# A recurrent-attention kernel: the carried state in a zero-padded layout, output matmuls all 64 columns wide, the two halves interleaved, and one gate moved forward on VectorE

## The chip, the cores and the metric

The kernel runs on one core of one Trainium2 chip. In the profiles PE is TensorE, DVE VectorE, ACT ScalarE and POOL GpSimd. The metric is the time of one execution on the device in microseconds (us), median over runs. The kernel before ran in 234.27 us (three runs, 232.32 to 235.18) when the prediction was made. One core has no second die to compare with, so a run counts as slow only where its time is over 1.5% above the fastest of its kernel; a single run is of unknown state. The figures inside one execution come from profiled executions; their span is about 1.8 us shorter than the time that is reported for the same run.

## The reference, cut to what matters

Per batch and head, a 48 x 48 state decays by `alpha`, takes in an outer product, and is read by `q`. The 384 outputs of a token (8 heads x 48) then go through a feed-forward layer with the activation h cos h.

```python
batch, n_heads, seq, head_dim = (4, 8, 768, 48)
for t in range(S):
    state = alpha[:, :, t, :, None] * state + np.einsum('bhd,bhe->bhde', k[:, :, t], v[:, :, t])
    y[:, :, t] = np.einsum('bhd,bhde->bhe', q[:, :, t], state)
...
h = x @ w_in          # 384 -> 2048
g = h * np.cos(h)
return (g @ w_out)    # 2048 -> 384
```

## The kernel before

The sequence is cut in 24 chunks of 128 tokens, 6 per batch. The recurrence within a chunk becomes matmuls; only the state goes from chunk to chunk. Head pairs share 128 contraction rows (two heads in slots of 64, 48 of them used). The state of a pair is 96 columns wide, so the state of all heads is 384 columns without gaps, the same layout as the output.

The output of a chunk is a 384 x 128 block, in three row groups (`kt`) of 128 partitions. Two sorts of matmul add up in it: the old state `U` against `q` ("U reads"), and `v` against the masked scores `A` ("v reads"). A v read is always 64 columns wide. A U read must not cross a pair, that is a multiple of 96, nor a 64-column tile, and so half of the U reads are only 32 columns wide:

```python
def state(j):                                   # "S": sum of k v over the chunk, plus the carry
    ...
    if not first:
        nc.tensor.matmul(t[:, 0 : NP * 96], ident_bf,
                         U_t[j - 1].rearrange("r p e -> r (p e)"), start=False, stop=True, ...)

def ev_state(j):                                # "u", on DVE
    t = work.tile([C, NP, 96], BF, tag="U_sb", bufs=3)
    nc.vector.tensor_tensor(out=t..., in0=U_ps.pop(j)..., in1=Em_t.pop(j)..., op=ALU.mult)
    U_t[j] = t

def outputs(j):                                 # "Y"
    ...
    for kt in range(3):
        if not first:
            U = U_t[j - 1].rearrange("r p e -> r (p e)")
            r = 0
            while r < C:
                f = kt * C + r
                p = f // 96
                n = min(96 * (p + 1), (kt + 1) * C, f - f % 64 + 64) - f     # 64 or 32
                mm(r, n, kt, U[:, f : f + n], qT[:, (NP + p) * C : (NP + p + 1) * C], True, False)
                r += n
        for r in range(2):
            for half in range(2):
                ...
                mm(64 * half, 64, kt, vs[:, c0 : c0 + 64],
                   A_t[j][:, ACOL[h] * C : (ACOL[h] + 1) * C], first and r == 0, r == 1)
```

The order in which each engine gets its work is written by hand, as a string of one-letter units per step. A step `s` works on chunk `s + 1` of the recurrence and on chunk `s` and `s - 2` of the feed-forward layer:

```python
units = {
    "T": transposes, "t": ev_transposes,        # TensorE; copy to SBUF on DVE
    "S": state, "u": ev_state,                  # TensorE; DVE
    "A": scores, "m": mask_scores,              # TensorE; DVE
    "Y": outputs, "y": ev_outputs,              # TensorE; DVE
    "0": ff1 first half, "1": ff1 second half,  # TensorE
    "i": act 0, "j": act 1,                     # ScalarE (sine)
    "p": gate 0, "r": gate 1,                   # DVE
    "2": ff2 first half, "3": ff2 second half, "e": ev_ff2, ...
}
elif s % 2 == 0:
    run(s, "o Tt 0i Su Am 2 1j Yyp r 3 e")
else:
    run(s, "o Tt 0i Su Am 2 1jp Yy r Pn 3 e C x")
```

## Time and profile before

| what | before |
|---|---|
| time | 234.27 us (232.32 to 235.18) |
| span of the profiled run | 235.5 us (its time was 237.25) |
| TensorE busy | 89% |
| one pair of steps without a first chunk (99.80 to 116.40 us) | 16.6 us |
| one output block of 20 matmuls, to the start of the next group | 1187 ns |
| wait of TensorE in each even step | 483 ns |

The profiled run, at 237.25 us, is 2.1% above the fastest run (232.32 us).

These lines are from the profile page of the kernel before: busy time by engine, the 40 slices of the span (tenths busy; PEclk is the granted TensorE clock in tenths), and the chain that ended last, by engine and by line.

```profile
span 235.5 us, 6142 instructions
PE 210.1 (89%) x2632; PEld 154.6 (66%) x2632; DVE 136.0 (58%) x160; ACT 124.7 (53%) x137; POOL 62.9 (27%) x104
...
PE   7858744877999999999999999999999999999983
...
PEclk9995985597999999999999999999999999999999
DMA  7999998991754777377268476843861561001001
...
PE 70%; DVE 18%; DMA 4%; ACT 2%; SPq 2%; issue 2%; ACTq 0%
```

From slice 11 on (about 60 us) TensorE stands at 9 and paces the kernel. The first 60 us have full DMA and a clock that comes and goes. DVE, on the chain with 18%, is busy for only 58% of the span, so the chain must hit it at a bad place. The timeline of DVE in an even step, and the longest wait of TensorE in the waits view (total us, times, longest), show where:

```profile
104.43 0.56 DVE L288 CAST t<-t 128x384 bf16<-128x384 f32 x1 [2.50 <-PE t L262]
104.90 2.35 DVE L317 TENSOR_TENSOR g_new<-t,c_sb 128x1024 bf16<-128x1024 f32 x2
107.16 0.68 DVE L199 COPY t<-t 128x1024 bf16<-128x1024 bf16 x1
...
PE t L233 <- DVE t L199: 7.4, 11, 3.7
```

DVE idles 2.5 us for the output block (unit Y), then runs y, both gates p and r, and only then the copy of the transposes (L199), for which the state matmuls (L233) wait. In nine even steps L233 starts 539 ns after the last ff1 matmul, where the matmul rate gives 56 ns.

The output block itself in the timeline of TensorE (start, length, instruction; the ends of matmuls are modelled, so read the starts):

```profile
103.14 0.41 PE L262 MATMUL t<-t 128*64 128x128 bf16 x3
103.47 0.30 PE L262 MATMUL t<-t,vpb 128*64 128x128 bf16 x4
103.61 0.22 PE L262 MATMUL t<-t 128*64 128x128 bf16 x2
103.66 0.28 PE L262 MATMUL t<-t,vpb 128*64 128x128 bf16 x4
103.87 0.41 PE L262 MATMUL t<-t 128*32 128x128 bf16 x3
104.04 0.35 PE L262 MATMUL t<-t,vpb 128*64 128x128 bf16 x4
104.32 1.47 PE L326 MATMUL o_new<-w_114,g_new 128*128 128x384 bf16 x8
```

The view merges neighbours (its first row holds one 64-wide and two 32-wide matmuls). The start stamps of the single matmuls in the same trace are finer. Columns: start in us, ns since the start before, width in columns, and what it is.

```
102.986   +55   128   (ff1)
103.136  +150    64   U
103.309  +173    32   U
103.312    +3    32   U
103.472  +160    64   v
103.476    +4    64   v
103.552   +76    64   v
103.556    +4    64   v
103.608   +52    64   U
...
103.872  +149    32   U
103.876    +4    32   U
104.036  +160    64   U
...
104.323  +152   128   (ff2)
```

Two matmuls on different halves start 3 or 4 ns apart, and the next pair follows 56 ns after. Every change of width takes 149 to 173 ns from start to start, and the first pair of 64-wide ones after it is followed by the next after 80 ns instead of 56. There are four changes inside the block (64 to 32 to 64, twice) besides the one into it and the one out of it.

### The profile page before, as it was taken

The numbers are of one execution on the slowest core, as the hardware profiler recorded it, in microseconds if no ns is written. First come the engines' busy times: TensorE is split into PE (matmuls) and PEld (weight loads), VectorE is DVE, ScalarE is ACT, GpSimd is POOL, SyncE is SP. The second block draws the span as 40 slices with busy tenths as digits, with TensorE's granted clock in tenths as the row PEclk, the third lists the DMA queues.
The fourth block names the chain that finished last, engine by engine and source line by source line (L and its number), as shares of the span: only waits on it lengthen the run. The fifth ranks groups of instructions, "written<-read, shape, count | busy, mean of one in ns | idle before, by whom it ended". The sixth has DMA issues, their size and how long they took to land.

```text
span 235.5 us, 6142 instructions
## 1 busy us (share of the span) xinstructions
PE 210.1 (89%) x2632; PEld 154.6 (66%) x2632; DVE 136.0 (58%) x160; ACT 124.7 (53%) x137; POOL 62.9 (27%) x104
## 2 busy tenths in 40 slices
PE   7858744877999999999999999999999999999983
PEld 2444642755786777777776867768777767778741
DVE  6535472293656738457557566486496566574620
ACT  4255407550594582863944945837729548323330
POOL 3220602650052080170250530800801605200000
PEclk9995985597999999999999999999999999999999
DMA  7999998991754777377268476843861561001001
GB/s 137 323 182 298 245 375 155 199 189 36 145 125 93 123 146 143 82 139 162 68 110 167 100 134 105 165 107 67 170 132 43 97 138 36 33 3 36 33 33 68
DMA packets 106203, 30.28 MB, mean 129 GB/s; under 512 B 100288, under 2 KB 105408, under 8 KB 106176
## 3 DMA queue, kind: packets, MB, share of 16 engines
q1 hardware_dynamic: 106176, 29.89, 59.5%
q8 instruction: 20, 0.33, 0.6%
q14 instruction: 7, 0.06, 0.1%
HBM read 25.17 MB, written 4.72 MB: 127 GB/s over the span
## 4 chain that ended last, share of the span: by engine, by line
PE 70%; DVE 18%; DMA 4%; ACT 2%; SPq 2%; issue 2%; ACTq 0%
PE o_new L326 23%; PE t L303 22%; DVE g_new L317 11%; PE t L262 11%; DMA a_new<-in_alpha_dram 4%; PE t L210 3%; PE t L193 3%; DVE t L199 3%; DVE t L288 3%; PE t L233 3%; PE cum_new L145 2%; PE t L239 2%; DVE w_114 L125 1%; DVE w_112 L115 1%; PE w_ps L338 1%
## 5 line engine op out<-in xcount | busy, mean ns | idle before, releaser
L310 ACT ACTIVATE c_sb<-t,halfpi 128x1024 bf16<-128x1024 f32 x48 | 53.5, 1114 | 63.1 <-PE t L303 62.7
L303 PE MATMUL t<-t,w_112 128*128 128x128 bf16 x1152 | 75.1, 224 | 1.0 <-DVE t L288 0.7
L326 PE MATMUL o_new<-w_114,g_new 128*128 128x384 bf16 x384 | 71.5, 331 | 3.9 <-DVE w_114 L125 2.8
L303 PEld LDWEIGHTS <-w_112 128*128 128x128 bf16 x1152 | 69.8, 100 | 4.5 <-DVE t L288 0.8
L317 DVE TENSOR_TENSOR g_new<-t,c_sb 128x1024 bf16<-128x1024 f32 x48 | 57.5, 1216 | 7.6 <-ACT c_sb L310 7.2
L174 POOL TENSOR_TENSOR khb<-t,icp_new 128x384 bf16<-128x384 f32 x24 | 24.0, 999 | 137.0 <-ACT icp_new L162 107.3
L326 PEld LDWEIGHTS <-g_new 128*128 128x128 bf16 x384 | 34.5, 98 | 28.3 <-issue 5.4
L288 DVE CAST t<-t 128x384 bf16<-128x384 f32 x24 | 13.4, 557 | 41.9 <-PE t L262 41.9
L219 DVE TENSOR_TENSOR t<-t,mask_f 128x1024 bf16<-128x1024 f32 x24 | 29.2, 1216 | 1.2 <-PE t L210 1.2
L331 ACT ACTIVATE o_sb<-o_new 128x384 f32<-128x384 f32 x24 | 11.6, 485 | 28.2 <-PE o_new L326 28.2
L245 DVE TENSOR_TENSOR t<-t,Em 128x384 bf16<-128x384 f32 x24 | 13.4, 558 | 21.3 <-PE t L239 17.2
L199 DVE COPY t<-t 128x1024 bf16<-128x1024 bf16 x24 | 16.5, 687 | 12.7 <-PE t L193 12.7
L176 POOL TENSOR_TENSOR qhb<-t,cp_new 128x384 bf16<-128x384 f32 x22 | 22.8, 1037 | 0.1
L262 PE MATMUL t<-t 128*64 128x128 bf16 (+1 forms) x160 | 21.2, 235 | 0.0
L262 PE MATMUL t<-t,vpb 128*64 128x128 bf16 x288 | 19.1, 229 | 0.0
L262 PEld LDWEIGHTS <-t 128*64 128x64 bf16 (+1 forms) x160 | 10.5, 102 | 7.5 <-issue 1.0
L233 PE MATMUL t<-vpb,khb 128*128 128x96 bf16 x96 | 8.5, 213 | 7.4 <-DVE t L199 7.4
L348 ACT ACT_TABLE_LOAD x11 | 14.1, 1283 | 0.9 <-PEq L448 0.7
L310 ACT ACT_TABLE_LOAD x11 | 14.1, 1283 | 0.2
L145 PE MATMUL cum_new<-lnab,triu_bf 128*128 128x384 bf16 x24 | 7.6, 343 | 7.3 <-ACT lnab L132 7.3
L132 ACT ACTIVATE lnab<-a_new 128x768 bf16<-128x768 f32 (+1 forms) x13 | 10.3, 793 | 6.4 <-DMA a_new<-in_alpha_dram 6.3
L178 POOL CAST vpb<-t 128x384 bf16<-128x384 f32 x24 | 13.1, 545 | 1.1 <-DMA t<-in_v_dram 0.6
(43 smaller groups left out, 145.4 us busy)
## 6 DMA issues: line engine op xcount, KB each, us to landing
a_new<-in_alpha_dram SPq DMA_DIRECT2D x24, 192.0 KB, 3.4
t<-in_k_dram SPq DMA_DIRECT2D x24, 192.0 KB, 3.8
t<-in_q_dram SPq DMA_DIRECT2D x24, 192.0 KB, 4.3
t<-in_v_dram SPq DMA_DIRECT2D x24, 192.0 KB, 4.2
out_dram<-o_sb SPq DMA_DIRECT2D x24, 192.0 KB, 2.0
w1f<-in_moe_w_in_dram SPq DMA_DIRECT2D x2, 1536.0 KB, 8.4
w2f<-in_moe_w_out_dram SPq DMA_DIRECT2D x2, 1536.0 KB, 10.9
```

Source lines behind the costliest of these rows:

```text
L174: nc.gpsimd.tensor_tensor(out=khb[:, j % 3, :, 0:D], in0=k_sb, in1=icp.rearrange("s (h d) -> s h d", h=H), op=ALU.mult)
L176: qeng.tensor_tensor(out=qhb[:, j % 3, :, 0:D], in0=q_sb, in1=cp[:, 0:HD].rearrange("s (h d) -> s h d", h=H), op=ALU.mult)
L199: nc.vector.tensor_copy(out=t, in_=qkT_ps.pop(j))
L219: nc.vector.tensor_tensor(out=t.rearrange("s (h t) -> s h t", h=H), in0=A_ps.pop(j).rearrange("s (h t) -> s h t", h=H), in1=mask_f.unsquee ...
L233: nc.tensor.matmul(t[:, p * 96 : (p + 1) * 96], khb[:, j % 3, 2 * p : 2 * p + 2].rearrange("s h d -> s (h d)"), vpb[:, j % 3, 2 * p : 2 * ...
L262: nc.tensor.matmul(t[r0 : r0 + n, kt * C : (kt + 1) * C], lhsT, rhs, start=start, stop=stop, skip_group_check=True)
L288: nc.vector.tensor_copy(out=t.rearrange("r k t -> r (k t)"), in_=y_ps.pop(j)[:, 0 : 3 * C])
L303: nc.tensor.matmul(t[:, f], w1[:, kk, ft * C : (ft + 1) * C], x_t[j][:, kk], start=(kk == 0), stop=(kk == 2))
L310: nc.scalar.activation(out=c_sb, in_=h_ps[j, half], func=AF.Sin, bias=halfpi, scale=1.0)
L317: nc.vector.tensor_tensor(out=g_t[j][:, half * HF : (half + 1) * HF], in0=h_ps.pop((j, half)), in1=c_t.pop((j, half)), op=ALU.mult)
L326: nc.tensor.matmul(o_ps[j][:, 0:DM], g_t[j][:, ft], w2[:, ft], start=(ft == 0), stop=(ft == NF - 1))
L348: nc.scalar.preload_act_table_set("natural_log_exp_and_others")
```

## The change

The state gets slots of 128 columns per pair, 96 used and 32 zero. A U read may then run over a pair's end into zeros, so all eight U reads can be 64 columns wide: a tile that spans two pairs is read twice, and each read adds zeros where the other has data. The number of matmuls stays 20. They are issued as two lists, one per half, in turn. In even steps the first gate p moves before the output block.

```diff
+    ub = consts.tile([C, 3, NP, C], BF, tag="ub")
+    nc.vector.memset(ub, 0.0)
...
     def ev_state(j):
-        t = work.tile([C, NP, 96], BF, tag="U_sb", bufs=3)
         nc.vector.tensor_tensor(
-            out=t.rearrange("r p (a e) -> r p a e", a=2),
+            out=ub[:, j % 3, :, 0:96].rearrange("r p (a e) -> r p a e", a=2),
...
+        U = ub[:, (j - 1) % 3].rearrange("r p e -> r (p e)")
+        mms = []
+        for T in range(2 * 3):
+            g, tt = T // 3, T % 3
+            a = []
             if not first:
+                for p, c0 in (((0, 0),), ((0, 64), (1, 96)), ((1, 160),))[tt]:
+                    c0 += 2 * C * g
+                    a.append((U[:, c0 : c0 + 64],
+                              qT[:, (NP + 2 * g + p) * C : (NP + 2 * g + p + 1) * C]))
             for r in range(2):
+                h = 4 * g + (2 * tt + r + 1) // 2
+                c0 = 4 * VS * g + 64 * (2 * tt + r)
+                a.append((vs[:, c0 : c0 + 64], A_t[j][:, ACOL[h] * C : (ACOL[h] + 1) * C]))
+            mms.append(a)
...
+        for i in range(max(len(mms[0]), len(mms[1]))):
+            for half in range(2):
+                if i < len(mms[half]):
+                    kt, start, stop, lhsT, rhs = mms[half][i]
+                    nc.tensor.matmul(t[64 * half : 64 * half + 64, kt * C : (kt + 1) * C], ...)
...
-            run(s, "o Tt 0i Su Am 2 1j Yyp r 3 e")
+            run(s, "o Tt 0i Su Am 2 1jp Yy r 3 e")
```

More of the change, by code (lines that the diff above doesn't have):

```diff
@@ L224, in mask_scores @@
         A_t[j] = t
-    U_ps, U_t = {}, {}
+    U_ps = {}
     def state(j):
@@ L238, in state @@
         if not first:
-            nc.tensor.matmul(t[:, 0 : NP * 96], ident_bf,
-                             U_t[j - 1].rearrange("r p e -> r (p e)"),
+            nc.tensor.matmul(t[:, 0 : NP * 96].rearrange("r (p e) -> r p e", p=NP), ident_bf,
+                             ub[:, (j - 1) % 3, :, 0:96],
                              start=False, stop=True, skip_group_check=True)
     def ev_state(j):
-        t = work.tile([C, NP, 96], BF, tag="U_sb", bufs=3)
         nc.vector.tensor_tensor(
-            out=t.rearrange("r p (a e) -> r p a e", a=2),
+            out=ub[:, j % 3, :, 0:96].rearrange("r p (a e) -> r p a e", a=2),
             in0=U_ps.pop(j)[:, 0 : NP * 96].rearrange("r (p a e) -> r p a e", p=NP, a=2),
@@ L249, in ev_state @@
         )
-        U_t[j] = t
     y_ps, x_t = {}, {}
@@ L259, in outputs @@
         qT = qkT_t[j]
-        def mm(r0, n, kt, lhsT, rhs, start, stop):
-            nc.tensor.matmul(t[r0 : r0 + n, kt * C : (kt + 1) * C], lhsT, rhs, start=start,
-                             stop=stop, skip_group_check=True)
-        for kt in range(3):
-            if not first:
-                U = U_t[j - 1].rearrange("r p e -> r (p e)")
-                r = 0
-                while r < C:
-                    f = kt * C + r
-                    p = f // 96
-                    n = min(96 * (p + 1), (kt + 1) * C, f - f % 64 + 64) - f
-                    mm(r, n, kt, U[:, f : f + n], qT[:, (NP + p) * C : (NP + p + 1) * C],
-                       True, False)
-                    r += n
-            for r in range(2):
-                for half in range(2):
-                    T = 2 * kt + half
-                    g, sl = T // 3, 2 * (T % 3) + r
-                    h = 4 * g + (sl + 1) // 2
-                    c0 = 4 * VS * g + 64 * sl
-                    mm(64 * half, 64, kt, vs[:, c0 : c0 + 64],
-                       A_t[j][:, ACOL[h] * C : (ACOL[h] + 1) * C], first and r == 0, r == 1)
+        U = ub[:, (j - 1) % 3].rearrange("r p e -> r (p e)")
@@ new lines, in outputs @@
+        for half in range(2):
+            mms[half] = [
+                (T // 2, i == 0, i == len(mms[T]) - 1) + m
+                for T in range(half, 6, 2) for i, m in enumerate(mms[T])
+            ]
+        for i in range(max(len(mms[0]), len(mms[1]))):
+            for half in range(2):
+                if i < len(mms[half]):
+                    kt, start, stop, lhsT, rhs = mms[half][i]
+                    nc.tensor.matmul(t[64 * half : 64 * half + 64, kt * C : (kt + 1) * C],
+                                     lhsT, rhs, start=start, stop=stop, skip_group_check=True)
@@ L291, in ev_outputs @@
         A_t.pop(j)
-        U_t.pop(j - 1, None)
     h_ps, g_t, o_ps = {}, {}, {}
```

## The prediction

> **What bounds the kernel.** From about 60 to 217 us TensorE sets the pace: in the 40 slices PE stands at 9, and the chain of waits runs mostly through it (PE 70%, DVE 18%). A pair of steps takes 16.6 us (state-carry matmul L239 at 99.80, then at 116.40). The first 60 us are mixed (DMA, casts, colder clock).
>
> **The output block (L262).** The starts of single matmuls in the trace show two 64-column matmuls on different halves starting 3 ns apart and pairs following every 56 ns; but where the column tile changes (128 to 64, 64 to 32, and back) the next start comes 149 to 173 ns later. The Trainium skill, "TensorEngine Tiling (Array Packing)", Key Properties, says that changing the tiling mode, not just the tile, drains the TensorE; the trace agrees. A 20-matmul block has four inner changes besides entry and exit; to the next group's start it takes 1187 ns in all 17 blocks after 62 us (timeline: 103.14 to 104.32). The 12-matmul block of a first chunk, all 64-column pairs already, takes 458 ns.
>
> **What changes.** (1) The 20 matmuls stay 20, all 64 columns wide, 10 per half, alternating. Estimate from the 458 ns block: 458 + 4 pairs x 56 = 682 ns. Each block saves 505 ns on the critical path: 17 blocks, 8.6 us. The three before 60 us give perhaps 0.9 us together.
> (2) In even steps DVE ran y, p, r and then the copy of the transposes (L199), which ended late: TensorE waits for it before L233 (waits view; 539 ns after the last ff1 matmul's start instead of 56, in 9 even steps: 4.3 us). With p before Y, p (1.22 us) runs while TensorE does ff1's second half, and the copy comes about 1.2 us earlier relative to Y, of which the shorter Y takes back 0.5 us. The wait should vanish: 4.3 us.
> (3) Added: a memset of the padded state on DVE, about 0.7 us (L69, equal size: 698 ns), before DVE waits 3.3 us for q: nothing. Strided state: nothing (L245 stays at 558 ns, L239 at 346 ns).
>
> **What could come back.** TensorE would need about 15.1 us per pair of steps; ACT and DVE are each busy a little over 10 us. The tightest chain: from odd steps ACT runs j, table load, ln, two exps, o_sb, table load, i without a break (111.52 to 119.0); then p on DVE. By my count p then ends just as y could start: at most 0.1 us of new wait a pair. DMA, busy 59.5% of the span, would reach 63%.
>
> **Sum.** 8.6 + 0.9 + 4.3 = 13.8 us, less 0.5 for new waits: 234.3 - 13.3 = 221.0 us. Range 218.5 to 224.0. Faster by over 2%: 0.96; within 2%: 0.03; slower: 0.01.
>
> **What the profile would show.** Right: L262 only as 128*64; 20-blocks of about 680 ns, no inner gap above 80 ns; no wait of L233 on L199 after 60 us; a pair of steps in 15.1 to 15.3 us; L245 and L239 unchanged; DVE below 10% of the chain. Wrong: blocks near 1 us (the halves do not overlap); a new wait of PE on L317, L288 or L199; a pair above 15.6 us.
>
> **What would make it wrong.** Accumulation from both halves at different column ranges of one bank serializing; the start shifting by a microsecond or two with the DMA; ACT or the input DMA not following the shorter step.

## The result, and the profile after

The changed kernel runs in 218.72 us (four runs, 218.52 to 220.73) against 234.73 us for the kernel before (four runs, 232.32 to 236.96; the slowest is 2.0% above the fastest, so it counts as slow, and the ratio is that of the other three). The ratio of the fast runs is 0.9369, with a 95% interval of 0.9270 to 0.9469. Such a ratio is the mean time of one kernel's fast runs over that of the other's of the same rounds, so it is not quite the ratio of the medians that are quoted. It is correct. The line numbers shift: L262 becomes L288 (output), L233 becomes L236 (state), L199 becomes L202 (copy), L303, L317 and L326 become L307, L321 and L330 (ff1, gates, ff2).

The same lines of the profile page as shown of before:

```profile
span 216.9 us, 6141 instructions
PE 193.0 (89%) x2630; PEld 147.9 (68%) x2632; DVE 135.9 (63%) x161; ACT 124.5 (57%) x137; POOL 62.4 (29%) x104
...
PE   6657653876999999999999999999999999999972
...
PEclk9999965699999999999999999999999999999999
DMA  7999999997765787489378575863863451101011
...
PE 82%; DVE 6%; DMA 4%; ACT 3%; SPq 2%; issue 2%; ACTq 0%; DVEq 0%
```

DVE falls from 18% of the chain to 6%, although it is busy as long as before (135.9 against 136.0 us). What remains in the chain is TensorE. The first, an inner and the last row of an output block, with the ff2 that follows:

```profile
101.91 0.25 PE L288 MATMUL t<-t,ub 128*64 128x128 bf16 x2
...
102.21 0.22 PE L288 MATMUL t<-t,vpb 128*64 128x128 bf16 x2
...
102.38 0.28 PE L288 MATMUL t<-t,vpb 128*64 128x128 bf16 x4
102.59 1.48 PE L330 MATMUL o_new<-w_116,g_new 128*128 128x384 bf16 x8
```

The block takes 681 or 682 ns in all 17 steady blocks (101.91 to 102.59). By the start stamps its inner gaps are 3 or 4, 77, and 52 or 53 ns, nothing longer. The even step on DVE, and the wait that remains:

```profile
94.44 1.23 DVE L321 TENSOR_TENSOR g_new<-t,c_sb 128x1024 bf16<-128x1024 f32 x1 [1.03 <-ACT c_sb L314]
95.58 0.55 DVE L293 CAST t<-t 128x384 bf16<-128x384 f32 x1
96.05 1.22 DVE L321 TENSOR_TENSOR g_new<-t,c_sb 128x1024 bf16<-128x1024 f32 x1
97.27 0.69 DVE L202 COPY t<-t 128x1024 bf16<-128x1024 bf16 x1
...
PE t L236 <- DVE t L202: 4.3, 2, 3.5
```

The gate p (94.44) now fills DVE's idle time before y (95.58). Of the eleven waits on the copy two remain, both before 60 us. The stretch from the fifth output block to the last one is the same work in both kernels, and the windows view of it (stretch, length, busy us of PE, PEld, DVE, ACT and POOL with numbers of instructions, clock, DMA share, GB/s) is the cleanest comparison. First before, then after:

```profile
62.53:216.97 154.44, 151.56 (x2060) 115.39 (x2058) 97.20 (x113) 93.40 (x101) 45.81 (x72) 1.00 0.52 105
```

```profile
57.03:198.94 141.91, 141.91 (x2060) 111.97 (x2059) 98.96 (x114) 93.32 (x101) 45.91 (x72) 1.00 0.56 114
```

The stretch is 12.53 us shorter, and by this view TensorE has no idle time left in it. The view goes by modelled ends, so short gaps like those at a change of width count as busy in both rows; the start stamps say the same of the wait, since the state matmuls now follow the last ff1 matmul by 55 or 56 ns in all 19 steps of the stretch. The tail after it is 0.51 us shorter (18.50 against 18.00 us), which is the last block. The first stretch, up to the fifth block, differs by 5.5 us in these two profiles (62.53 against 57.03 us); whether the change did that is a question for the experiments.

### The profile page after: what moved, and what is told of

The parts are those of the page before. It is cut to its first block, busy times and chain, and to the rows that moved or that the text cites. A ratio compares the mean times of both kernels' runs of the same rounds, so it can differ in the third digit from the quotient of the medians.

```text
span 216.9 us, 6141 instructions
## 1 busy us (share of the span) xinstructions
PE 193.0 (89%) x2630; PEld 147.9 (68%) x2632; DVE 135.9 (63%) x161; ACT 124.5 (57%) x137; POOL 62.4 (29%) x104
## 3 DMA queue, kind: packets, MB, share of 16 engines
q1 hardware_dynamic: 106176, 29.89, 64.6%
## 4 chain that ended last, share of the span: by engine, by line
PE 82%; DVE 6%; DMA 4%; ACT 3%; SPq 2%; issue 2%; ACTq 0%; DVEq 0%
PE o_new L330 30%; PE t L307 30%; PE t L288 7%; PE t L196 5%; DMA a_new<-in_alpha_dram 4%; PE t L213 3%; DVE g_new L321 3%; PE cum_new L148 2%; PE t L236 2%; PE t L242 2%; DVE t L222 1%; SPq L100 1%; PE cum_new L152 1%; ACT lnab L135 1%; DVE w_116 L128 1%
## 5 line engine op out<-in xcount | busy, mean ns | idle before, releaser
L307 PE MATMUL t<-t,w_114 128*128 128x128 bf16 x1152 | 73.9, 222 | 0.9 <-DVE t L293 0.9
L330 PE MATMUL o_new<-w_116,g_new 128*128 128x384 bf16 x384 | 70.3, 327 | 4.2 <-DVE w_116 L128 3.1
L307 PEld LDWEIGHTS <-w_114 128*128 128x128 bf16 x1152 | 68.9, 99 | 4.2 <-DVE t L293 1.1
L321 DVE TENSOR_TENSOR g_new<-t,c_sb 128x1024 bf16<-128x1024 f32 x48 | 58.4, 1218 | 18.1 <-ACT c_sb L314 17.7
L330 PEld LDWEIGHTS <-g_new 128*128 128x128 bf16 x384 | 34.2, 98 | 28.0 <-issue 4.9
L247 DVE TENSOR_TENSOR ub<-t,Em 128x384 bf16<-128x384 f32 x24 | 13.4, 558 | 23.9 <-PE t L242 18.7
L202 DVE COPY t<-t 128x1024 bf16<-128x1024 bf16 x24 | 16.6, 690 | 10.2 <-PE t L196 10.2
L179 POOL TENSOR_TENSOR qhb<-t,cp_new 128x384 bf16<-128x384 f32 x22 | 22.1, 1003 | 0.1
L293 DVE CAST t<-t 128x384 bf16<-128x384 f32 x24 | 13.3, 554 | 13.3 <-PE t L288 13.3
L288 PE MATMUL t<-t,vpb 128*64 128x128 bf16 x288 | 16.0, 224 | 0.4 <-DVE t L222 0.4
L288 PEld LDWEIGHTS <-vpb 128*64 128x64 bf16 x288 | 13.2, 112 | 0.7 <-issue 0.4
L288 PE MATMUL t<-t,ub 128*64 128x128 bf16 x160 | 13.4, 230 | 0.0
L152 PEld LDWEIGHTS <-lnab 128*128 128x128 bf16 x96 | 5.5, 98 | 10.9 <-issue 8.9
```

The lines of the kernel that those rows point to most:

```text
L179: qeng.tensor_tensor(out=qhb[:, j % 3, :, 0:D], in0=q_sb, in1=cp[:, 0:HD].rearrange("s (h d) -> s h d", h=H), op=ALU.mult)
L202: nc.vector.tensor_copy(out=t, in_=qkT_ps.pop(j))
L247: nc.vector.tensor_tensor(out=ub[:, j % 3, :, 0:96].rearrange("r p (a e) -> r p a e", a=2), in0=U_ps.pop(j)[:, 0 : NP * 96].rearrange("r ( ...
L288: nc.tensor.matmul(t[64 * half : 64 * half + 64, kt * C : (kt + 1) * C], lhsT, rhs, start=start, stop=stop, skip_group_check=True)
L293: nc.vector.tensor_copy(out=t.rearrange("r k t -> r (k t)"), in_=y_ps.pop(j)[:, 0 : 3 * C])
L307: nc.tensor.matmul(t[:, f], w1[:, kk, ft * C : (ft + 1) * C], x_t[j][:, kk], start=(kk == 0), stop=(kk == 2))
```

## The experiments

The theory has two independent parts: (a) TensorE pays for each change of column width, and (b) TensorE waited for a copy that stood behind a gate in the DVE queue. Rivals: the gain comes from the alternation of the halves or from the padding as such; the two parts overlap, or one wait only turns into another; the shorter first 60 us are part of the effect. The table gives all runs; the block is the steady output block of 20 matmuls, the pair is two steady steps, and the stretch goes from the fifth to the last output block.

| run | median us (runs) | ratio to before | block ns | pair us | stretch us | 5th block starts at us |
|---|---|---|---|---|---|---|
| before, first profile | 234.27 (3) | | 1187 | 16.59 | 154.44 | 62.53 |
| before_again | 234.39 (1) | | 1187 | 16.59 | 154.44 | 59.64 |
| changed kernel | 218.72 (4) | 0.9369 | 682 | 15.09 | 141.91 | 57.03 |
| after_again | 220.52 (4) | 0.9380 | 682 | 15.09 | 141.91 | 59.14 |
| order_only | 229.42 (5) | 0.9741 | 1187 | 16.10 | 150.00 | 60.26 |
| layout_only | 224.66 (4) | 0.9624 | 682 | 15.59 | 146.39 | 59.76 |
| tile_order | 220.33 (4) | 0.9401 | 682 | 15.09 | 141.91 | 60.02 |
| one_switch (wrong result) | 220.66 (4) | 0.9446 | 740 | 15.21 | 142.86 | 57.42 |
| one_switch_marks | 222.83 (1) | | 740 | 15.21 | 142.85 | 60.12 |
| three_switches | 226.89 (1) | | 1017 | 15.76 | 147.28 | 59.47 |
| half_by_half | 227.06 (1) | | 1043 | 15.81 | 148.14 | 58.75 |
| carry_dve | 217.92 (4) | 0.9275 | 682 | 14.76 | 139.31 | 58.66 |

One of the five runs of order_only and one of the four of tile_order, and two of the runs of before beside them, counted as slow by their time; the ratios leave these out, the medians in the table do not. Runs of one execution have no interval, so their times are not compared. All these verdicts rest on the block and the stretch, where the granted clock is 1.00 and which repeat to 0.02 us between profiles of the same kernel.

### Only the order of DVE's work

```diff
 (the kernel before)
-            run(s, "o Tt 0i Su Am 2 1j Yyp r 3 e")
+            run(s, "o Tt 0i Su Am 2 1jp Yy r 3 e")
```

> The kernel before with only the order in even steps changed (the gate of the first half before the output block). If the wait of the state matmuls on the copy of the transposes came from the gate's place in the DVE queue: the output block stays at 1187 ns, the gap from the last ff1 matmul to the state matmuls falls from 539 to about 56 ns in the 9 even steps, a pair of steps takes 16.6 - 0.48 = 16.1 us, and the time falls by about 4.3 us against the kernel before. Rival (the wait only moves to another buffer or engine): the pair stays near 16.6 us and the time within 1 us of before.

The block stays at 1187 ns, the steady wait is gone and the stretch falls by 4.44 us (154.44 to 150.00). The waits view of this run keeps only the two early waits:

```profile
PE t L233 <- DVE t L199: 4.3, 2, 3.5
```

The ratio is 0.9741 (0.9644 to 0.9839), that is 2.6% or some 6 us. The stretch's 4.44 us are 1.9% and lie inside the interval, so the surplus is no finding; the start, taken up below, varies by as much. Part (b) is shown alone, in its predicted size, and the wait did not move elsewhere.

### Only the layout and the width

```diff
 (the changed kernel)
-            run(s, "o Tt 0i Su Am 2 1jp Yy r 3 e")
+            run(s, "o Tt 0i Su Am 2 1j Yyp r 3 e")
```

> The changed kernel with the old order in even steps. If the two parts are independent: block 682 ns, the 483 ns wait of the state matmuls is still there in 9 even steps, a pair of steps takes 16.6 - 1.0 = 15.6 us, and the time is about 4.3 us above the changed kernel, 223 us. Rival (the shorter block alone already takes the wait away, or makes it longer because the copy now comes later against TensorE): a pair at 15.1 us, or above 15.9 us.

```profile
PE t L236 <- DVE t L202: 7.2, 11, 3.5
```

The block takes 682 ns, and all eleven waits on the copy are back. The stretch is 8.05 us shorter than before. The reason that the wait is neither longer nor shorter lies in the order: y, p, r and the copy on DVE all start from the end of the output block, and so does TensorE's work up to the state matmuls. A shorter block moves both sides by the same time: the state matmuls start 540 to 545 ns after the last ff1 matmul here, against 538 to 540 ns before. The two parts add up: 4.44 + 8.05 = 12.49 us against 12.53 us for both together. The median lies 5.9 us above the changed kernel's first 218.72 us, but that also holds a difference of starts; the stretch gives 4.48 us.

### Sixty-four columns, but in the old order of tiles

```diff
 (the changed kernel, outputs)
-        for i in range(max(len(mms[0]), len(mms[1]))):
-            for half in range(2):
-                ...                        # the two halves in turn
+        for kt in range(3):
+            pair = (mms[2 * kt], mms[2 * kt + 1])
+            seq = [(half, i) for half in range(2) for i in range(len(pair[half]) - 2)]
+            seq += [(half, len(pair[half]) - 2 + r) for r in range(2) for half in range(2)]
+            for half, i in seq:
+                ...                        # U reads of both halves, then v reads in turn
```

> The changed kernel, padded state and 64-column matmuls, but issued tile by tile in the old order instead of as two alternating streams; a half then has two matmuls in a row in three places. If only the column width matters and each half works off its own queue: the block stays at 682 to 740 ns and the time within 1 us of the changed kernel. Rival (the alternation of the halves is what gives the overlap): two neighbours on one half cost a full 56 ns each with nothing beside them, 3 x 56 = 170 ns more or worse, block 850 ns or above, time 3 us or more above the changed kernel.

The block takes 682 ns and the stretch 141.91 us, to the last digit what the changed kernel has. The strict alternation, half of the change's name, is worth nothing here. The program has two places with two neighbours on one half, not three as was expected. They do no harm, because the matmul after them is on the other half and can overlap with the second of them: in the start stamps the block is still ten pairs, 3 or 4 ns within a pair. The stamps also show the U and v reads in exactly the order of the changed kernel, in all 17 blocks, although the program has another: in four of the pairs the matmul that comes later in the program starts first, by 3 or 4 ns.

### All of one half, then all of the other

```diff
 (the changed kernel, outputs)
-        for i in range(max(len(mms[0]), len(mms[1]))):
-            for half in range(2):
+        for half in range(2):
+            for i in range(len(mms[half])):
```

> The changed kernel, same matmuls and operands, but all ten of one half first and then all ten of the other. If matmuls start in program order and only neighbours on different halves overlap: about 18 starts at 56 ns and one pair, block 79 + 17 x 56 + 3 + 152 = about 1190 ns, which is as slow as the kernel before without any change of width; a pair of steps about 16.1 us. Rival (the queue pulls matmuls of the other half forward by itself, so the order of issue is of no account): 682 ns and 15.1 us.

Neither number came. The block takes 1043 ns: 361 ns more than 682, but 147 ns less than the 1190 ns of strict order. The timeline shows why (the names `ub` and `vpb` tell a U read from a v read):

```profile
105.58 0.24 PE L288 MATMUL t<-t,ub 128*64 128x128 bf16 x1
...
105.83 0.28 PE L288 MATMUL t<-t,vpb 128*64 128x128 bf16 x2
...
105.94 0.30 PE L288 MATMUL t<-t,ub 128*64 128x128 bf16 x4
...
106.05 0.30 PE L288 MATMUL t<-t,vpb 128*64 128x128 bf16 x4
```

In program order the first half ends with U, U, v, v and the second begins with U, U, v, v. The trace has four U reads in a row and then four v reads: the matmuls of the second half began while three of the first half had not started. By the start stamps the second half's first matmul starts 5 ns after the seventh of the first half, and from there both halves run at 56 ns each until the first is done. So the queue does run ahead to a free half, but by three matmuls and not by ten. The 12-matmul blocks of this run agree: there the second half starts 6 ns after the third of six, again with three still to come. The order was not changed before the run: the program holds all ten of one half before those of the other. Why it is three, no run tests. Keeping the halves close together in the program matters; strict turns do not.

### Unpadded, but with the narrow matmuls first

```diff
 (the kernel before with the new order in even steps, outputs)
-        (per kt: U reads 64 or 32 wide, then v reads, issued at once)
+        (collected as narrow[kt] and wide[kt]; w0, w2 the four v reads of kt 0 and 2;
+         u the two 64-wide U reads of kt 0 and 2)
+        for m in narrow[0] + narrow[2] + u + wide[1] + w0 + w2:
+            mm(*m)
```

> The unpadded state of the kernel before, 32-column and 64-column matmuls as before, but all four 32-column matmuls first, then the 64-column ones; the new order in even steps. Same 20 matmuls, one inner change of width instead of four. If each change costs about 150 to 160 ns as the starts suggest: block about 740 ns (0 + 9 + 160 + 79 + 6 x 56 + 3 + 152), a pair of steps about 15.2 us, time about 1 us above the changed kernel. Rival (the padding or the evenness of the streams matters, or 32-column weight loads are slow in themselves): block stays above 950 ns.

The block takes 740 ns, as the sum of the gaps said. The timeline of one block and the ff2 after it (the first row holds the four 32-wide U reads and the four 64-wide ones, which it merges):

```profile
102.59 0.47 PE L262 MATMUL t<-t 128*32 128x128 bf16 x8
102.90 0.50 PE L262 MATMUL t<-t,vpb 128*64 128x128 bf16 x12
103.33 0.34 PE L333 MATMUL o_new<-w,g_new 128*128 128x384 bf16 x1
```

The result is wrong (relative error 0.14), which does not alter what a block costs but makes the kernel no candidate. Its cause was tested at the end, below. What follows for (a): with the same unpadded state and the same 32-wide matmuls, grouping takes 447 of the 505 ns. The padding itself, beyond grouping, is worth 58 ns per block. That is 4 narrow matmuls in 9 ns plus one change of 160 ns, against two more pairs of 56 ns.

### Three changes instead of one

```diff
-        for m in narrow[0] + narrow[2] + u + wide[1] + w0 + w2:
+        for m in narrow[0] + u + wide[1] + narrow[2] + w0 + w2:
```

> As the run with one change of width (unpadded state, new order in even steps), but the 32-column matmuls in two places, so three inner changes. If the cost goes by the number of changes: block about 4 + 160 + 194 + 149 + 4 + 160 + 194 + 152 = 1017 ns. Rival (32-column matmuls are slow in themselves, whatever stands beside them): about 740 ns as with one change. The start marks are set so that the result should be correct: only the first matmul on each quarter of the output partitions clears.

The block takes 1017 ns, again to the nanosecond of the sum, and the result is correct. One block in the timeline, where the second group of 32-wide reads stands apart:

```profile
98.40 0.47 PE L262 MATMUL t<-t 128*32 128x128 bf16 x6
98.70 0.28 PE L262 MATMUL t<-t,vpb 128*64 128x128 bf16 x4
98.91 0.23 PE L262 MATMUL t<-t 128*32 128x128 bf16 x2
99.07 0.41 PE L262 MATMUL t<-t,vpb 128*64 128x128 bf16 x8
99.42 1.48 PE L333 MATMUL o_new<-w,g_new 128*128 128x384 bf16 x8
```

The matmuls are those of the run above; their places differ, and the start marks, which were put right here. (The next run changes the marks alone, and the block keeps its 740 ns.) So 32-wide matmuls are not slow in themselves; the changes between widths are. Blocks by inner changes: none 682, one 740, three 1017, four 1187 ns.

### The wrong result

```diff
 (the unpadded kernel with the narrow matmuls first; start mark of the U reads)
-                         True, False))
+                         (kt, r) in ((0, 64), (0, 96), (2, 0), (2, 32)), False))
```

> The run with one change of width, whose result was wrong, with one difference: the start mark stands only on the first matmul on each quarter of the output partitions. If the wrong result came from start marks that cleared sums still pending in other columns of the same bank: correct now, block 740 ns as in that run. Rival (32-column outputs ahead of the rest are wrong for another reason, a race): wrong again.

It is correct now, with the block at 740 ns. So the wrong result came from the start marks and not from a race: every U read had cleared, also where sums of other columns on the same partitions were pending. The Trainium skill, "PSUM — Partial Sum Buffer", The four PSUM rules, says that a start mark clears, over the whole bank on the partition quarters it writes, the bits that make a later matmul add to a sum instead of overwriting it; the two runs agree (error 0.14 with marks on all U reads, correct with one per quarter). The changed kernel is safe because each half finishes one tile before it starts the next.

### A version that beats both

If TensorE has no idle time and DVE has, the next step is to give TensorE's work away. The carry of the state is an identity matmul of 384 columns; DVE can add it while it evacuates the state.

```diff
 (the changed kernel, abridged)
     def state(j):
...
-        if not first:
-            nc.tensor.matmul(t[:, 0 : NP * 96]..., ident_bf, ub[:, (j - 1) % 3, :, 0:96], ...)
     def ev_state(j):
+        u = U_ps.pop(j)...
+        if j % NC != 0:
+            s_sb = work.tile([C, NP, 96], FP, tag="s_sb")
+            nc.vector.tensor_tensor(out=s_sb..., in0=u, in1=ub[:, (j - 1) % 3, :, 0:96]..., op=ALU.add)
+            u = s_sb...
         nc.vector.tensor_tensor(out=ub[:, j % 3, :, 0:96]..., in0=u, in1=Em..., op=ALU.mult)
```

> A version meant to beat both: the changed kernel with the carry of the state taken from TensorE (identity matmul, 384 columns) to DVE (one more pass over the state). If TensorE alone sets the pace of the changed kernel and DVE has room: the carry's 162 ns leave each of 20 steps, a pair of steps 15.1 - 0.32 = 14.8 us, time about 3 us below the changed kernel. Rival (DVE, now busy 63% and with its gate just in time, becomes the limit): pair at 15.1 us or above with waits of TensorE on DVE.

It runs correctly in 217.92 us against 220.52 us for the changed kernel in the same rounds (ratios to before 0.9275, interval 0.9196 to 0.9354, and 0.9380, interval 0.9324 to 0.9436). The intervals overlap by a little, though the runs do not (216.54 to 219.40 against 219.60 to 221.22 us); the gain is about 1%. The profiles settle it: the pair falls from 15.09 to 14.76 us and the stretch from 141.91 to 139.31 us, that is by 2.60 us, or 16 carries of 162 ns. The windows view of a steady part (columns as above) shows TensorE still without idle time, with DVE at 108.55 of 138 us (the added pass takes 558 ns, the one after it 652 ns):

```profile
62.00:200.00 138.00, 138.00 (x2022) 110.13 (x2020) 108.55 (x130) 91.04 (x100) 48.68 (x72) 1.00 0.56 116
```

### Does the start vary by itself?

> The changed kernel once more, beside the kernel before on the same chip. If the first 60 us vary by themselves: pair of steps again 15.09 us, stretch from the 5th to the last output block again 141.9 us, while the 5th output block starts anywhere from 56.5 to 61 us. If the change itself had shortened the first 60 us by over 3 us: 5th block at 57 to 58 us in this run too and all times near 218.6 us.

> The kernel before, profiled again. If its steady part is fixed and the first 60 us vary: block 1187 ns, pair of steps 16.6 us, 5th to last output block 154.4 us as in the first profile; the 5th output block starts not at 62.5 us but earlier, about 58 to 61 us, and the time is about 232 to 236 us. Rival (the kernel before always starts slowly): 5th block at 62 us or later.

The steady figures repeat: 154.44 us twice for before, 141.91 us twice for after. The start of the fifth block does not: 62.53 and 59.64 us in two profiles of the same kernel before, 57.03 and 59.14 us in two of the changed kernel, and 57.42 to 60.26 us in the eight other variants. (The 62.53 us are those of the run that is slow by its time.) The 5.5 us between the first two profiles were mostly two different starts and not an effect of the change. In the stretches shown above the granted clock is 1.00; before 60 us it dips, at other times in each profile (the PEclk rows of the two pages). If the steady parts are taken as fixed, an estimate for the seven runs of before in the last timed rounds puts the fifth block at 60.5 us on average (mean time 235.26, less 1.8, less 154.44, less 18.5), and for the four runs of after_again at 58.8 us (mean time 220.47, less 1.8, less 141.91, less 18.0). The change may have shortened the start by one or two microseconds; the runs do not settle it, nor what sets the start's length in one run.

## Why the prediction was right

- **The time.** 221.0 us was predicted, with 218.5 to 224.0; 218.72 us was measured, and 220.52 us in later rounds. Both are in the range. The first lies only 0.22 us above its lower edge: that the mechanism gives about 13 us and the first medians differ by 16 is a matter of the start, and that the time stayed inside the range was partly luck.
- **The block.** Predicted: 682 ns from the 458 ns block of a first chunk and four more pairs. Measured: 681 or 682 ns in 17 of 17. The step held because the kernel already contained the new block in small: a first chunk's block is all 64 columns wide. Seventeen times 505 ns is 8.6 us; layout_only shows 8.05 us in the stretch (16 of the 17 blocks).
- **The reason for it.** Changes of width were named, and one_switch and three_switches show it; the alternation and the padding as such are excluded by tile_order and one_switch. The Trainium skill's statement in "TensorEngine Tiling (Array Packing)", Key Properties, that a change of mode drains the TensorE, agrees with the 149 to 173 ns gaps here.
- **The wait.** Predicted: 4.3 us vanish. Measured: 4.44 us alone (order_only), and no wait on the copy after 60 us. The prediction said that the shorter block "takes back 0.5 us" of the copy's lead. That size was off. In layout_only, where DVE is free at the block's end, the copy and the state matmuls both count from there and nothing is taken back. In the changed kernel DVE is still at p then, and y starts about 0.28 us after ff2's start instead of 0.11, so about 0.17 us is lost (0.39 us in three of the steps). The copy still ends 0.32 to 0.45 us before the state matmuls start; where TensorE waited for it, in the kernel before, that was 0.06 us.
- **New waits.** Predicted: 0.5 us. Measured: none on TensorE; it counts as busy for 141.91 of 141.91 us, and no state matmul waits. The tight place that was named is visible: p ends just when y could start, and y starts 0.27 us after ff2's start in the even step shown (95.58 against 95.31), where the odd step has 0.11 us (102.70 against 102.59). It costs nothing here, since the copy behind it keeps the margin just named.
- **The start.** Predicted: 0.9 us. The runs neither confirm nor refute it; the start varies by more than that. The three blocks themselves took 6.32 and 5.97 us together in the two profiles of before, 5.36 and 5.66 us in the two of the changed kernel, with waits that differ from run to run.
- **The sum.** Predicted: 13.3 us. The stretch and the tail give 12.53 + 0.51 = 13.04 us in the first pair of profiles and 0.03 us more in the second. That this is so near 13.3 is in part luck: the 0.9 us for the start is not shown and the 0.5 us for new waits did not come, and the two nearly cancel. The mean times of the later rounds differ by 14.8 us (235.26 against 220.47). The 16.0 us between the first two medians hold luck in the start.
- **Other signs.** L262 as L288 appears only as 128*64; the pair is 15.09 us (15.1 to 15.3 predicted); L245 as L247 stays at 558 ns, L239 as L242 is at 336 ns against 346 ns; DVE has 6% of the chain (below 10% predicted); DMA is at 64.6% (63% predicted).

## What to carry to other kernels

Price a block of small matmuls by the gaps between single starts, not by busy time, and look in the same trace for a place where the wanted form already runs; its rate is the best estimate there is. Put matmuls of one tile width together before changing the layout: order alone gave 447 of the 505 ns here, the padding the last 58, and strict turns between the halves none, as long as both halves appear within a few instructions of each other. On an engine that is off the critical path, fill its idle time before the event with work that is ready, so that what must follow the event follows at once.

## What the Trainium skill lacked or had wrong

- "TensorEngine Tiling (Array Packing)", Key Properties, says that a change of mode drains the TensorE, but gives no size. Here a change between 128, 64 and 32 columns takes 149 to 173 ns from start to start, where pairs follow every 56 ns without one. A change of rows shows in the trace of the changed kernel too: the score matmuls (48 rows) start 258 ns after the 384-column carry, where the 384-column matmuls of ff2 follow each other after 162 or 163 ns (the second after 173).
- "TensorE: Matmul & The Clock Gate", Part 3, says that matmuls start and end in program order ("strict FIFO, no reordering"). The trace of half_by_half shows otherwise for starts on two column halves: the second half's first matmul starts 5 ns after the seventh of the first half, with three still to come, and the block takes 1043 ns where strict order would give about 1190 ns.
- The same page gives the queue's depth and says that weight loads are pulled ahead, but no page says how far ahead of earlier matmuls one may start on a free tile. In half_by_half it was three matmuls, in blocks of 20 and of 12.
